# Two product banks lent to the score visits of the w_out stages

## The chip, the cores and the metric

The kernel runs on one core of a Trainium2 chip. The metric is device time in microseconds (us), and the median of the kernel before is 370.91 us over three runs (370.6, 370.91, 370.95). Names: TensorE is PE in the profile (its weight loads are PEld), VectorE is DVE, ScalarE is ACT, GpSimd is POOL, SyncE is SP. PSUM is the memory that TensorE writes; here it is used as eight banks, each holding 512 float32 values on each of the 128 partitions.

## The reference

Squared-ReLU attention is followed by a two-layer network with squared ReLU. There are 8 batches, 12 heads, 448 positions and a head width of 64; the model width is 768 and the inner width 2048.

```python
scores = scale * np.matmul(q, k.transpose(0, 1, 3, 2))
attn = np.maximum(scores, 0.0) ** 2 / S
attn_out = np.matmul(attn, v)
x = attn_out.transpose(0, 2, 1, 3).reshape(B * S, H * D)
r = np.maximum(x @ w_in, 0.0)
return (r * r) @ w_out
```

## The kernel before

**Work and stages.** Attention is cut into 24 units of four heads (three units for each batch), and each unit into 7 score tiles of 128 x 896. A score tile is four quarter-array matmuls at 448 columns (`score`, matmul at L262). ScalarE takes it out of PSUM with a ReLU (L266), VectorE squares it (L369), and when a unit has its seven tiles an AV unit of 28 quarter-array matmuls (`av_unit`, L317) multiplies them by v; ScalarE evicts its result into x (L323).

The first two batches go through w_in as plain products (`h_group`, L409), six matmuls for each of 16 column groups. Then stages alternate: a w_out stage for each pair of batches (four of them, with 3, 4, 3 and 4 groups: 14 in all), and between them the w_in stage of the next pair, with two periods for each batch (12 periods in all).

**A w_in period** (`h_period`, matmuls at L538) is a seven-product scheme on two sets, 14 products of six matmuls. Each set s has two accumulators, X (index 0) and Y (index 1). The tuple `order` names for each product its set, its number in the scheme, its accumulator, whether it starts afresh, and what is done at its end. Counted from 0:

- product 0: set 0, X, copied by ScalarE (L475); 1: set 1, X, copied;
- 2: set 0, Y, summed by VectorE (`plus`, L481); 3: set 0, X, copied; 4: set 1, X, copied; 5: set 1, Y, summed;
- 6: set 0, Y, copied; 7: set 0, X, summed; 8: set 1, X, copied; 9: set 1, Y, summed;
- 10 and 11: sets 0 and 1, X, evicted by ScalarE with a ReLU (L490); 12 and 13: sets 0 and 1, Y, summed by VectorE.

Squares of g by VectorE (L487) lie between. A product that isn't fresh goes on adding into what its accumulator holds.

**A w_out group** (`o_groups`, matmuls at L725) is a seven-product scheme for two row tiles, with products of eight matmuls and two accumulators, X and Y. Its list of products, counted from 0, is (accumulator, fresh, left, right, end):

```python
(X, True, lambda: tile_of(rows[0])[:, LO], b11, end1),
(Y, True, lambda: tile_of(rows[0])[:, HI], b21, end2),
(X, False, lambda: ss[2], t2, end6),
(Y, True, lambda: ss[1], t1, end5),
(X, False, lambda: ss[3], t3, end7),
(X, False, lambda: tile_of(rows[1])[:, HI], nt4, end4),
(Y, False, lambda: ss[4], b22, end3))
```

After product 0 ScalarE copies X (L627); after 1 VectorE adds that copy to Y (L632); after 2 ScalarE copies X; after 3 nothing is read; after 4 ScalarE copies X and VectorE adds the copy to Y; after 5 ScalarE evicts X (L675); after 6 VectorE adds to Y. The next group's product 0 is placed between products 4 and 5. At the end of a stage that another follows, a w_in product of the next stage stands in that place. In the last group of all, product 5 has an accumulator Z in the other pair, and product 6 is cut in two (L707).

**PSUM.** The pool `s_p` holds two score slots of two banks each. The pools in `big`, called mma and mmb, have two buffers of one bank each. `mm_tile(i)` takes a fresh one-bank tile from pool i, and without i from the two pools in turn. A w_in period takes set 0's X and Y from one pool and set 1's from the other. A w_out group n takes both of its accumulators from pool n % 2, so that the other pool is free from the end of the group before until the next group's product 0.

**Order.** The order of instructions on each engine is the order in which the code issues them, and the framework puts in the semaphore waits from what each tile is read and written by. The main loop at the end walks a list `steps` of matmuls with their assumed costs and keeps a `clock`; a list of `events` has due times. In front of a product, where `edge` is true, events that are due are fired. A `visit` is one such event: it issues two score tiles, and an AV unit after the first tile if one is due. 21 visits for each of the last three pairs of batches are spread evenly by due time over the stretch ahead of the w_in stage that needs them. VectorE's squares wait in a list `due` and are put by assumed times of TensorE and VectorE (`fill`, `flush`).

Of the kernel before, what the change touches and what calls it, by code (L numbers as in the profile page):

```python
# [12 lines left out]
FP32 = mybir.dt.float32  # L13
# [5 lines left out]
def kernel(  # L19
# [12 lines left out]
    NT, DM = out.shape  # L32
# [10 lines left out]
    P = 128  # L43
    J = 7
    PW = S // J
    NU = 3
    NUN = B * NU
# [23 lines left out]
    PSUM = bass.MemoryType.PSUM  # L71
# [122 lines left out]
    def slot(dtype, third=False):  # L194
        return (third_p if third else s_p).tile(
            [P, 2, 2048 // mybir.dt.size(dtype)], dtype, name="slot", tag="slot")
# [54 lines left out]
    now = [0]  # L251
    avt = [None]

    def score(t, times=1, third=False):
        n, j = divmod(t, J)
        qT, kT = qkt[n]
        ps = slot(FP32, third)
        for hh in list(range(2)) * times:
            r = slice(64 * hh, 64 * hh + 64)
            for hp in range(2):  # L260
                c = slice(64 * hp, 64 * hp + 64)
                nc.tensor.matmul(  # L262
                    ps[c, hh, 0:S], lhsT=kT[r, j, c], rhs=qT[r, :, c],
                    start=True, stop=True)
        at = at_p.tile([P, 2, S], FP16, name="at", tag="at")
        nc.scalar.activation(out=at, in_=ps[:, :, 0:S], func=AF.Relu, scale=SK)  # L266
        ats[t] = at
        seen[t] = now[0]
# [29 lines left out]

    unit = [NU]

    def av_unit():

        n = unit[0]
        if n == NUN or seen.get(n * J + J - 1, 10 ** 6) >= now[0]:
            return
        unit[0] += 1
        flush(rest=False)
        at_pe[0] += 1.33
        b, u = divmod(n, NU)
        vt = vts[n]  # L310
        ps = slot(FP32)
        for j in range(J):
            at = ats.pop(n * J + j)
            for hp in range(2):
                r = slice(64 * hp, 64 * hp + 64)
                for hh in range(2):
                    nc.tensor.matmul(  # L317
                        ps[64 * hh:64 * hh + 64, hp, 0:S],
                        lhsT=vt[r, hh, j * D:(j + 1) * D], rhs=at[r, hh, :],
                        start=(j == 0), stop=(j == J - 1))  # L320
        if u == 0:
            xts[b] = x_p.tile([P, NM, S], FP16, name="xt", tag="xt")
        nc.scalar.activation(  # L323
            out=xts[b][:, 2 * u:2 * u + 2, :], in_=ps[:, :, 0:S],
            func=AF.Copy, scale=CX)

    def prefetch(m):
        if m >= NUN:
            return
        dma_transpose(m)  # L330
        if m > NPE:
            load_v(m)
        if m + 2 < NUN:
            load_qk(m + 2)
# [10 lines left out]
    def flush(rest=True):  # L345
        for d in (due, due_g) if rest else (due,):
            while d:
                put(d)

    def put(d):  # L350
        ready, cost, fn, _ = d.popleft()
        at_ve[0] = max(at_ve[0], at_pe[0], ready) + cost
        fn()

    def fill(until):
        for d in (due, due_g):
            while d and max(at_ve[0], at_pe[0], d[0][0]) + d[0][1] <= until:
                put(d)
# [8 lines left out]
    def square(at, lag=0.0):  # L367
        due.append((at_pe[0] + lag, 0.54,
                    lambda: nc.vector.tensor_mul(at, at, at), 0))  # L369

    def visit(tiles):
        now[0] += 1
        for t in tiles:
            if t % J == 0 and t >= NPE * J:
                prefetch(t // J + 2)
        for t in tiles[:1]:
            score(t)
        av_unit()
        for t in tiles[1:]:
            score(t)  # L380
        at_pe[0] += 0.19 + 0.19 * len(tiles)
        for i, t in enumerate(tiles):
            square(ats[t], 0.6 + 0.85 * i)
# [2 lines left out]
    gts: dict = {}  # L386
    mm_no = [0]

    def mm_tile(i=None, dtype=FP32):
        if i is None:  # L390
            mm_no[0] += 1
            i = mm_no[0] % len(big)
        return big[i].tile(
            [P, 2048 // mybir.dt.size(dtype)], dtype, name="mm", tag="mm")

    def g_of(b):
        if b // 2 not in gts:
# [42 lines left out]
    def sums_x(b, i):  # L440
        xt = xts[b]
        lo, hi = slice(0, NH), slice(NH, NM)
        b11, b12, b21, b22 = (xt[:, lo, 0:Q], xt[:, lo, Q:S], xt[:, hi, 0:Q],
                              xt[:, hi, Q:S])
        now_ve(0.42)
        if i != 2:
            t = late["xs"].tile([P, NH, Q], FP16, name=f"x{i}", tag=f"x{i}")
            xsum[b, i] = t
        if i == 0:
            nc.vector.tensor_sub(t, b12, b11)  # L450
        elif i == 1:
            nc.vector.tensor_sub(t, b22, xsum[b, 0])
        elif i == 2:
            nc.vector.tensor_sub(b12, b22, b12)
        else:
            nc.vector.tensor_sub(t, b21, xsum[b, 1])
# [139 lines left out]
    def o_groups(groups, then):  # L596
# [5 lines left out]
        def group(n, rows, last):  # L602
# [7 lines left out]
            def needs(k):  # L610

                return max(2 * p + (tb > 2) for p, tb in groups[k]
                           if (p, tb) not in saved)

            def ahead(i, k=n):
                if k < len(groups) and i not in sets[k]:
                    flush_g(needs(k))
                    sums(i, groups[k], sets[k])
# [95 lines left out]
            def step(k, f):  # L714
                acc, fresh, left, right, end = products[k]
                if last and k == 5:
                    acc, fresh = Z, True

                def run():
                    if f == 0 and fresh and k != 3:  # L720
                        acc[:] = [mm_tile((n + (k == 5)) % 2)]
                    if f == 0 and k == 0:
                        ahead(1)
                        ahead(2)
                    nc.tensor.matmul(  # L725
                        acc[0][:, 0:HALF], lhsT=left()[:, f], rhs=right[:, f],
                        start=(fresh and f == 0),
                        stop=(f == KH - 1), skip_group_check=not fresh)
                    if f == KH - 1:
                        end()  # L730
                        if k < 4 and n + 1 < len(groups):
                            some = sum(d[3] <= needs(n + 1) for d in due_g)
                            for _ in range(-(-some // (4 - k))):
                                put(due_g)
                        fill(at_pe[0] + AFTER[k])
                return run

            ls = [[(0.1625, step(k, f), ((2 if k == 5 else True) if f == 0 else False))
                   for f in range(KH)] for k in range(7)]
            if last:  # L740
                ls[6] = [(0.0825, step3(z, f), False) for z in range(2) for f in range(KH)]
# [2 lines left out]
        def pre(i):  # L744
            sums(i, groups[0], sets[0])

        lists = [group(n, rows, rows == LAST) for n, rows in enumerate(groups)]
        for n, ls in enumerate(lists):
            for k in range(7):
# [26 lines left out]
    NB0 = NU * J  # L776
    ps = slot(FP32, True)
# [3 lines left out]
    def s(t, times=2):  # L781
# [73 lines left out]
    load_qk(7)  # L855
    first.close()
    big.append(ctx.enter_context(tc.tile_pool(
        name="mma", bufs=2, space=PSUM, reuse_waits="tile")))

# [2 lines left out]
    def some(part):  # L864
        for _, fn, _ in part:
            fn()
# [6 lines left out]
    some(f1[0:4])  # L873
    rounds.close()
    big.append(ctx.enter_context(tc.tile_pool(
        name="mmb", bufs=2, space=PSUM, side="right", reuse_waits="tile")))
    some(f0[4:6])
    visit([NB0, NB0 + 1])

# [6 lines left out]
    events = []  # L886
# [22 lines left out]
    for m in (6, 7):  # L909
        events.append((T_H + (1 + 3 * (m - 6)) * T_G, lambda m=m: prefetch(m)))  # L910
    at0 = T_H + 8 * T_G
    for pr in range(1, B // 2):
        t0 = 2 * NB0 * pr
        end = begin[pr] + T_S - 6.5
        gap = (end - at0) / 21
        for i in range(21):
            ts = [t0 + 2 * i, t0 + 2 * i + 1]
            events.append((at0 + i * gap, lambda ts=ts: visit(ts), True))
        at0 = end
        for i in range(4):  # L920
            events.append((begin[pr] - 6 + i, lambda b=2 * pr, i=i: sums_x(b, i)))
    events.append((at0 + 0.3, lambda: visit([]), True))

    def pre(pr, i):
        def run():
# [29 lines left out]
                steps += periods[b, i0]  # L955
        steps += outs[pr][0]

    clock, last = 0.0, 0.0
    ev = deque(sorted(events, key=lambda e: e[0]))
    for cost, fn, edge in steps:  # L960
        fired = 0
        while ev and edge and ev[0][0] <= clock + (1.6 if edge == 2 and not fired else 1e-3):
            if len(ev[0]) == 3:
                if clock < last + 1.5:
                    break
                last = clock
            ev.popleft()[1]()
            fired += 1
        if fn is not None:
            at_pe[0] += cost  # L970
            fn()
        clock += cost
# [31 lines left out]
```

## Time and profile before

| what | value |
| --- | --- |
| median of three runs | 370.91 us |
| profiled execution, its own time | 370.7 us |
| its span | 368.9 us |
| granted TensorE clock | 0.998 |
| TensorE busy | 359.6 us |
| VectorE busy | 265.4 us |
| ScalarE busy | 247.5 us |
| GpSimd busy | 107.1 us |

The span is the time from the first to the last instruction that the profiler saw; the profiled execution's own time is 1.8 us longer. A row of a group of instructions gives the source line, the engine, the operation, what it writes and reads, how often, its busy time and the mean of one. Some rows that later steps use:

| line | engine and what it does | times | mean, ns |
| --- | --- | --- | --- |
| L266 | ACT, eviction of a score tile, 128 x 896 | 168 | 925 |
| L323 | ACT, eviction of an AV unit, 128 x 896 | 21 | 917 |
| L475 | ACT, copy in a w_in period, 128 x 448 | 72 | 552 and 554 |
| L481 | DVE, sum in a w_in period, 128 x 448 | 72 | 622 and 619 |
| L627 | ACT, copy in a w_out group, 128 x 384 | 42 | 492 and 494 |
| L632 | DVE, sum in a w_out group, 128 x 384 | 44 | 542 and 556 |
| L369 | DVE, square of a score tile, 128 x 896 | 147 | 617 |

In the timeline, an entry begins with its start in us and its length in us; a matmul's end is modelled, so the start of the next matmul tells better when TensorE was free. In brackets stand the idle time before an instruction and what ended it.

### The profile page before, as it was taken

How to read it: one execution, taken by the hardware profiler on the slowest of the kernel's cores; microseconds unless marked ns; L12 is line 12 of the kernel's file. 1: busy time of each engine (PE TensorE's matmuls, PEld its weight loads, DVE VectorE, ACT ScalarE, POOL GpSimd, SP SyncE). 2: the span in 40 equal slices, each digit the busy share in tenths (PEclk: the TensorE clock that was granted, in tenths of full speed). 3: DMA queues.
4: the chain of work that ended last, by engine and by line, in shares of the span. 5: the costliest groups of instructions: out<-in, count | busy, mean ns of one | idle time of the engine just before them, and what ended most of it. 6: DMA issues, size and time to landing. Idle time of an engine off the chain costs nothing.

```text
span 368.9 us, 8720 instructions
## 1 busy us (share of the span) xinstructions
PE 359.6 (97%) x3588; PEld 230.3 (62%) x3588; DVE 265.4 (72%) x470; ACT 247.5 (67%) x371; POOL 107.1 (29%) x128
## 2 busy tenths in 40 slices
PE   8899999999999999999999999999999999999994
PEld 3644445445555778875555588786555689976663
DVE  2997677997777787788585766989766686884442
ACT  3988894787676989876556588886765885532220
POOL 8545521846553155531225045140000000000001
PEclk9999999999999999999999999999999999999999
DMA  8999999999999999967699899692323300003333
GB/s 115 191 207 203 205 204 162 161 158 165 190 166 127 184 101 98 115 93 62 140 166 105 159 155 86 88 116 37 65 71 88 85 3 2 2 0 85 87 92 81
DMA packets 121159, 42.64 MB, mean 116 GB/s; under 512 B 100832, under 2 KB 117760, under 8 KB 121120
## 3 DMA queue, kind: packets, MB, share of 16 engines
q0 software_dynamic: 82912, 23.01, 62.3%
q1 hardware_dynamic: 38048, 18.98, 25.7%
q8 instruction: 28, 0.46, 0.5%
q10 hardware_dynamic: 160, 0.10, 0.1%
q14 instruction: 11, 0.09, 0.1%
HBM read 45.61 MB, written 11.01 MB: 153 GB/s over the span
## 4 chain that ended last, share of the span: by engine, by line
PE 90%; ACT 3%; DVE 3%; issue 2%; DMA 1%; POOL 0%; POOLq 0%; ACTq 0%
PE mm L725 34%; PE mm L538 27%; PE slot L262 10%; PE mm L409 9%; PE slot L317 7%; ACT at L266 3%; DMA k<-in_k_dram 1%; DVE at L297 1%; PE avt L280 1%; PE slot L238 1%; PE mm L238 0%; DVE at L369 0%; DVE xt L292 0%; ACT u L627 0%; DVE osb L632 0%
## 5 line engine op out<-in xcount | busy, mean ns | idle before, releaser
L266 ACT ACTIVATE at<-slot 128x896 f16<-128x896 f32 x168 | 145.8, 925 | 22.2 <-PE slot L262 22.2
L369 DVE TENSOR_TENSOR at<-at 128x896 f16<-128x896 f16 x147 | 87.1, 617 | 9.7 <-ACT at L266 9.6
L109 POOL DMA_DIRECT2D qs<-in_q_dram x36 | 35.3, 983 | 113.7 <-DMA qT<-qs 106.2
L725 PEld LDWEIGHTS <-s 128*128 128x128 f16 x440 | 41.5, 98 | 32.7 <-issue 3.6
L262 PE MATMUL slot<-qT,kT 64*64 64x448 f16 x744 | 56.8, 361 | 1.9 <-ACT at L266 1.4
L538 PEld LDWEIGHTS <-w 128*128 128x128 f16 x576 | 54.3, 98 | 5.1 <-issue 4.3
L538 PE MATMUL mm<-xt,w 128*128 128x224 f16 x432 | 48.9, 259 | 0.0
L725 PEld LDWEIGHTS <-g 128*128 128x128 f16 x336 | 31.7, 98 | 24.1 <-issue 4.7
L538 PEld LDWEIGHTS <-ws 128*128 128x128 f16 x432 | 40.3, 98 | 4.7 <-issue 4.7
L632 DVE SCALAR_TENSOR_TENSOR osb<-mm,u 128x384 f32<-128x384 f32 (+1 forms) x30 | 16.2, 542 | 36.4 <-ACT u L627 24.0
L725 PE MATMUL mm<-b,g 128*128 128x384 f16 x224 | 40.7, 326 | 0.0
L725 PE MATMUL mm<-b,s 128*128 128x384 f16 x216 | 39.6, 326 | 0.2 <-DVE s L594 0.2
L409 PE MATMUL mm<-xt,w 128*128 128x448 f16 x192 | 39.8, 354 | 0.0
L725 PE MATMUL mm<-t,s 128*128 128x384 f16 x224 | 39.3, 326 | 0.0
L109 POOL DMA_DIRECT2D ks<-in_k_dram x36 | 35.1, 976 | 9.4 <-DMA b<-in_moe_w_out_dram 5.8
L262 PEld LDWEIGHTS <-kT 64*64 64x64 f16 x744 | 19.0, 104 | 28.7 <-issue 23.3
L561 POOL DMA_DIRECT2D out_dram<-osb x2 | 1.1, 563 | 119.6 <-DVE osb L632 119.6
L627 ACT ACTIVATE u<-mm 128x384 f32<-128x384 f32 x28 | 13.8, 492 | 31.6 <-PE mm L725 27.1
L538 PE MATMUL mm<-x,ws 128*128 128x224 f16 x288 | 34.1, 259 | 0.0
L481 DVE CUSTOM_DVE_ANT_0 g<-mm,m 128x448 f16<-128x448 f32 x36 | 22.4, 622 | 15.1 <-PE mm L538 7.3
L317 PE MATMUL slot<-at,vt 64*64 64x448 f16 x588 | 31.9, 350 | 0.2 <-DVE at L369 0.2
L409 PEld LDWEIGHTS <-w 128*128 128x128 f16 x192 | 17.1, 98 | 19.2 <-issue 5.1
(76 smaller groups left out, 399.7 us busy)
## 6 DMA issues: line engine op xcount, KB each, us to landing
out_dram<-osb SPq DMA_DIRECT2D x52, 192.0 KB, 3.0
vt<-in_v_dram POOLq DMA_DIRECT2D x24, 224.0 KB, 6.2
qs<-in_q_dram POOLq DMA_DIRECT2D x36, 112.0 KB, 4.6
ks<-in_k_dram POOLq DMA_DIRECT2D x36, 112.0 KB, 5.0
w<-in_moe_w_in_dram POOLq DMA_DIRECT2D x8, 384.0 KB, 11.9
b<-in_moe_w_out_dram POOLq DMA_DIRECT2D x4, 768.0 KB, 17.1
q<-in_q_dram POOLq DMA_DIRECT2D x6, 224.0 KB, 7.9
k<-in_k_dram POOLq DMA_DIRECT2D x6, 224.0 KB, 8.3
```

What stands on the lines that cost most here:

```text
L109: nc.gpsimd.dma_start(out=t[:, :, hh, :], in_=heads(src, n)[:, hh].rearrange("p (j d) -> p j d", d=D))
L238: nc.tensor.transpose(pss[i][64 * hh:64 * hh + 64, i if n < 4 else 0, j * P:(j + 1) * P], src[:, hh, j * D:(j + 1) * D], ident)
L262: nc.tensor.matmul(ps[c, hh, 0:S], lhsT=kT[r, j, c], rhs=qT[r, :, c], start=True, stop=True)
L266: nc.scalar.activation(out=at, in_=ps[:, :, 0:S], func=AF.Relu, scale=SK)
L317: nc.tensor.matmul(ps[64 * hh:64 * hh + 64, hp, 0:S], lhsT=vt[r, hh, j * D:(j + 1) * D], rhs=at[r, hh, :], start=(j == 0), stop=(j == J - 1))
L369: lambda: nc.vector.tensor_mul(at, at, at), 0))
L409: nc.tensor.matmul(cell[0][:, 0:S], lhsT=w1[f // 4][:, m, (f % 4) * P:(f % 4 + 1) * P], rhs=xts[b][:, m, :], start=(m == 0), stop=(m == NM ...
L481: nc.vector._custom_dve(TENSOR_ADD_SAT, out=gs(s, hi, right), in0=acc(s, y), in1=keep[s, nm], s0=3.4e38, s1=0.0)
L538: nc.tensor.matmul(XY[s][y][:, r * Q:(r + 1) * Q], lhsT=left(k, i0 + 2 * s + r, m), rhs=right(k, m), start=(fresh and r == 0 and m == 0), ...
L627: nc.scalar.activation(out=t, in_=X[0][:, 0:HALF], func=AF.Copy, scale=CO)
L632: nc.vector.scalar_tensor_tensor(out=osb[row][:, c], in0=acc[0][:, 0:cc.stop - cc.start], scalar=CO, in1=keep[nm][:, cc], op0=ALU.mult, op ...
L725: nc.tensor.matmul(acc[0][:, 0:HALF], lhsT=left()[:, f], rhs=right[:, f], start=(fresh and f == 0), stop=(f == KH - 1), skip_group_check=n ...
```

## The change

The change has three parts. First, each pair of product banks is no longer a pool of two one-bank buffers but **one tile of two banks**, taken once for the whole kernel. `mm_tile` returns one half of it, and the halves alternate (`side`). Second, `visit`, `score` and `av_unit` take an optional place `spare`: if an AV unit is due it goes there, otherwise the visit's first score tile does. Third, the visits of the last three pairs are no longer events at fixed times. The main loop counts the tiles that are issued (`tile_no`) against the plan (`planned`), and fires a visit at an edge where the count has fallen to the plan. At the edges of products 2 and 4 of a w_out group, a visit has three tiles and gets the pair that the group doesn't use, as soon as it is at most 1.5 tiles ahead of the plan; elsewhere it has two, as before.

In the built programs, there are 76 calls of `visit` before (63 of them and one without tiles in the last three pairs) and 67 after. 18 of the 67 have three tiles, and all 18 are in w_out stages. The number of matmuls doesn't change, nor does the order of transfers on the SP and POOL queues.

```diff
-    def score(t, times=1, third=False):
+    def score(t, times=1, third=False, ps=None):
...
-        ps = slot(FP32, third)
+        ps = slot(FP32, third) if ps is None else ps
...
-    def av_unit():
+    def av_due():
         n = unit[0]
-        if n == NUN or seen.get(n * J + J - 1, 10 ** 6) >= now[0]:
+        return n < NUN and seen.get(n * J + J - 1, 10 ** 6) < now[0]
+
+    def av_unit(ps=None):
+        if not av_due():
             return
...
-        ps = slot(FP32)
+        ps = slot(FP32) if ps is None else ps
...
-    def visit(tiles):
+    def visit(tiles, spare=None):
...
         for t in tiles[:1]:
-            score(t)
-        av_unit()
+            score(t, ps=None if av_due() else spare)
+        av_unit(spare)
...
+    side = [0, 0]
     def mm_tile(i=None, dtype=FP32):
...
-        return big[i].tile(
-            [P, 2048 // mybir.dt.size(dtype)], dtype, name="mm", tag="mm")
+        side[i] ^= 1
+        return big[i][:, side[i]].bitcast(dtype) if dtype != FP32 else big[i][:, side[i]]
...
-            ls = [[(0.1625, step(k, f), ((2 if k == 5 else True) if f == 0 else False))
+            edges = {2: (n + 1) % 2, 4: (n + 1) % 2}
+            ls = [[(0.1625, step(k, f),
+                    ((edges.get(k), k == 5) if f == 0 else False))
                    for f in range(KH)] for k in range(7)]
...
     big.append(ctx.enter_context(tc.tile_pool(
-        name="mma", bufs=2, space=PSUM, reuse_waits="tile")))
+        name="mma", bufs=1, space=PSUM, reuse_waits="tile")).tile(
+            [P, 2, 512], FP32, name="mma", tag="mma"))
...
     big.append(ctx.enter_context(tc.tile_pool(
-        name="mmb", bufs=2, space=PSUM, side="right", reuse_waits="tile")))
+        name="mmb", bufs=1, space=PSUM, side="right", reuse_waits="tile")).tile(
+            [P, 2, 512], FP32, name="mmb", tag="mmb"))
...
-        gap = (end - at0) / 21
-        for i in range(21):
-            ts = [t0 + 2 * i, t0 + 2 * i + 1]
-            events.append((at0 + i * gap, lambda ts=ts: visit(ts), True))
+        plan.append((at0, end, t0))
...
-    events.append((at0 + 0.3, lambda: visit([]), True))
...
+        while ev and edge and ev[0][0] <= clock + 1e-3:
+            ev.popleft()[1]()
+        if edge and clock >= plan[0][0]:
+            pair, soon = edge if edge is not True else (None, False)
+            ahead = tile_no - planned(clock)
+            if tile_no == NT:
+                if unit[0] < NUN and clock > last + 1.5:
+                    visit([])
+                    last = clock
+            elif pair is not None and ahead <= 1.5 and clock > last + 1.25:
+                n = min(3, NT - tile_no)
+                visit(list(range(tile_no, tile_no + n)), big[pair])
+                tile_no += n
                 last = clock
-            ev.popleft()[1]()
-            fired += 1
+            elif ahead <= (1.5 if soon else 0.0) and clock > last + 1.5:
+                n = min(2, NT - tile_no)
+                visit(list(range(tile_no, tile_no + n)))
+                tile_no += n
+                last = clock
```

The new functions and lines move the ones below them: in the kernel after, L323 is L327, L369 is L373, L409 is L418, L475 is L484, L481 is L490, L490 is L499, L538 is L547, L594 is L603, L627 is L636, L632 is L641, L675 is L684 and L725 is L734.

## Prediction

> **What bounds the kernel now.** I read the page first, then the waits of TensorE, the chain that ended last, and two stretches of the timeline.
>
> ```profile
> PE 359.6 (97%) x3588; PEld 230.3 (62%) x3588; DVE 265.4 (72%) x470; ACT 247.5 (67%) x371; POOL 107.1 (29%) x128
> ...
> PE 90%; ACT 3%; DVE 3%; issue 2%; DMA 1%; POOL 0%; POOLq 0%; ACTq 0%
> ```
>
> TensorE (PE) is busy in 97% of the span and is 90% of the chain. This is all that its matmuls wait for:
>
> ```profile
> PE slot L262 <- ACT at L266: 1.4, 6, 0.3
> PE slot L200 <- DVE zeros L158: 1.2, 1, 1.2
> PE slot L238 <- ACT at L266: 0.5, 2, 0.2
> PE slot L262 <- DVE kT L215: 0.2, 1, 0.2
> PE mm L725 <- DVE s L594: 0.2, 1, 0.2
> PE slot L317 <- DVE at L369: 0.2, 1, 0.2
> ```
>
> That is 3.7 us, and the product lines L538 and L725 have 0.2 of it. So the time is TensorE's own work: the change gains what it takes off TensorE and loses whatever makes TensorE wait. The chain prices a visit, and the wake-up of TensorE after another engine:
>
> ```profile
> 80.31 2.71 PE mm L725 x16
> 83.02 0.50 PE slot L262 x8
> 83.52 2.71 PE mm L725 x16
> ...
> 204.64 0.61 DVE s L594
> 205.25 0.05 issue
> 205.30 1.47 PE mm L725 x8
> ```
>
> Two score tiles take 0.50 us, and the 16 matmuls beside them 2.71. The timeline of the last w_out stage, which has no visits, shows how evictions lie beside products today:
>
> ```profile
> 338.97 2.76 PE L725 MATMUL mm<-t,s 128*128 128x384 f16 x16
> 339.23 0.56 DVE L632 SCALAR_TENSOR_TENSOR osb<-mm,m 128x384 f32<-128x384 f32 x1 [0.80 <-PE mm L725]
> 340.52 0.49 ACT L627 ACTIVATE u<-mm 128x384 f32<-128x384 f32 x1 [3.46 <-PE mm L725]
> 341.57 1.46 PE L725 MATMUL mm<-b,s 128*128 128x384 f16 x8
> ```
>
> These 16 matmuls are products 2 (in bank X) and 3 (in bank Y) of a group; they take 341.57 - 338.97 = 2.60 without a pause. VectorE reads product 1 out of Y while product 2 runs in X, and ScalarE reads product 2 out of X while product 3 runs in Y. The same in a w_in period:
>
> ```profile
> 322.67 0.74 PE L538 MATMUL mm<-x,ws 128*128 128x224 f16 x6
> 323.24 1.31 PE L538 MATMUL mm<-xt,w 128*128 128x224 f16 x12
> 323.44 0.54 ACT L475 ACTIVATE m<-mm 128x448 f32<-128x448 f32 x1 [0.61 <-PE mm L538]
> 324.12 0.62 DVE L481 CUSTOM_DVE_ANT_0 g<-mm,m 128x448 f16<-128x448 f32 x1 [0.53 <-ACT m L475]
> ```
>
> Product 6 ends at 323.24 in Y; its eviction starts 0.20 later, while product 7 already runs in X.
>
> [...]
>
> **Part 1: fewer visits.** The built orders have 76 visits before and 67 after, with the same matmuls (3588). A tile is 0.19 us (28 matmuls, seven tiles' worth, are 1.32 us in the chain). A visit's own cost is 0.50 - 2 x 0.19 = 0.12 at its entry and 2.71 - 2.60 = 0.11 at its exit: 0.23. Nine fewer: **-2.1 us**. The two 0.2 us waits in products and AV units lie in crowded places that the new plan thins out: -0.4.
>
> **Part 2: one tile for two banks.** Before, every accumulator is a tile of its own, from a pool of two. After, each pair is one tile for the whole kernel, and `mm_tile` returns a half. The framework sets waits by tile. I followed each wait in the two built programs to the instruction that brings the semaphore to the awaited count: before, no product waits on a reader of another bank; after, 123 products at L547 (the old L538), 58 at L734 (old L725) and 23 at L418 (old L409) wait on the reader of **the other half of their pair**. So a product that ran beside its neighbour's eviction now waits for it. These are no new instructions, only the cover that is gone. Behind the waiting matmul stands everything that TensorE has left.
>
> Price of such a wait, when the eviction belongs to the product just ahead: by ScalarE 0.20 (release, above) + 0.55 (rows L475: 552 and 554 ns) + 0.05 (wake-up) = 0.80; by VectorE 0.20 + 0.62 (rows L481) + 0.05 = 0.87. With one product of 0.576 between, 0.22 and 0.29.
>
> w_in period, 14 products. Product 3 waits for VectorE's sum of 2 (0.87); 5, 7 and 9 for ScalarE's copies of 4, 6 and 8 (3 x 0.80); 11 for the sum of 9 (0.29); 13 for relu of 11 (0.22); the next period's 0 and 1 for the sums of 12 and 13 (together 0.30). Product 2's wait for the copy of 0 is covered, since 1 was late; 4, 6, 8, 10 and 12 find their releases done. Sum 4.08. In VectorE's new order squares that wait for products 10 and 11 stand ahead of the last two sums: about 0.45 more. 12 periods: 12 x 4.53 = **+54.4**.
>
> w_out group, 7 products; the next group's product 0 runs in the other pair between 4 and 5. Product 2 waits for VectorE's sum of 1: 0.26 + 0.56 + 0.05 = 0.87. Product 3 waits for ScalarE's copy of 2: 0.25 + 0.49 + 0.05 = 0.79. Product 5 waits for copy and sum after 4: 0.26 + 0.49 + 0.14 + 0.56 + 0.05 = 1.50, of which the next group's product covers 1.30: 0.20. Product 6 waits for the copy of 5: 0.20 + 0.50 + 0.05 = 0.75. Sum 2.61; 14 groups: **+36.5**. In each of the four stages the first product 1 follows its product 0 directly (4 x 0.74 = 3.0), and in three the last group has a w_in product of 0.576 where 1.30 was (3 x 0.73 = 2.2): **+5.2**.
>
> First batches (L409): each half is freed one group of 1.14 us ahead, and an eviction takes 0.80. Between 0 and 4 us; I take +1.
>
> **Part 3: visits among these waits.** A visit ahead of a waiting product is hidden in its wait; but ScalarE works in order, and a visit's evictions (0.925 each) stand ahead of the next copy. In w_out, three tiles ahead of product 2 hide its 0.87, and then 2.78 us of evictions delay the copy that product 3 now waits for: 0.35 + 2.78 + 0.54 = 3.67 after the visit's start instead of 2.1 + 0.79, some 0.8 more: even. Ahead of product 4, with about half of the 18 visits of three, the copy and the sum that product 5 waits for end some 0.8 later with nothing hidden: 9 x 0.8 = 7; the two-tile visits hide about 1: **+6**. In w_in stages 25 visits either hide some 0.6 (ahead of 3, 5, 7, 9) or push a copy back by up to 1.2 (ahead of 4, 10): near even, with squares in front of VectorE's sums **+4**. Not seen in any trace: bounds from -12 (each visit hidden wherever it can be) to +20 (each pushes one eviction).
>
> The three-tile visit itself needs no wait: spare is free when it starts (last reader one product back or more), and its eviction ends before the pair's next product. POOL and SP queues get the same transfers in the same order around moved visits; their landing is far from the chain (no DMA in it after the start).
>
> **Sum**, on the profiled execution's 370.7 us (span 368.9 and 1.8 around it; the runs' median is 370.91, as good as equal): -2.1 - 0.4 + 54.4 + 36.5 + 5.2 + 1 + 6 + 4 = +104.6, so **475 us**. The release latency may be 0.1 off in 100 direct waits (10 us), and part 3 has its bounds.
>
> **Rivals.**
> - *Half the waits are covered* (423 us, half of 104): visits and late evictions overlap more than the walk through one period shows, as ScalarE and VectorE have over 28% of the span free. Against it: the last four w_out groups and most of the last three w_in periods have no visits at all, and there nothing can cover.
> - *The waits don't bind, only the visits count* (370.7 - 2.5 = 368.2 us, not slower). Place: products 3, 5, 7, 9 and 2, 3, 6. It decides if the release a product waits for belongs to an earlier reader than I took, so that it comes before TensorE arrives: with more than 0.80 us of other TensorE work between, no wait is left. The counts in the built program speak against it.
> [...]
>
> **Numbers.** Main case 0.86, half covered 0.07, no binding 0.03, pile-up 0.04. The main case's own bounds are 440 to 500; inside lies some 0.8 of all, so that is the range. Within 0.2% is about what the runs can tell from no change. Slower by more than 0.2%: main, half and pile-up, 0.97; within: 0.01; faster: 0.02.
>
> **What would show it.** In the after profile, the waits of TensorE list L547 on ACT L484 and DVE L490 and L734 on ACT L636 and DVE L641, together some 90 to 100 us where it was 0.2; PE's share near 77% with busy time near 358; a timeline in which product 7 starts 0.8 after product 6 ends; the last w_out stage, 37 us from 327 on, some 10 us longer. The visit count's saving shows as 67 entries. Wrong would be: those waits under 20 us in sum, or a granted clock under 0.95.

## Result and profile after

The kernel after takes **462.19 us** (median of four runs, 462.13 to 463.85) against 370.81 us before (also four runs): a ratio of 1.2476, 95% interval 1.2447 to 1.2504. It is slower by 91.4 us; the forecast was 475 us, range 440 to 500. The profiled execution has 462.18 us, a span of 460.4 us and a granted clock of 0.998.

The page of the kernel after, parts 1 and 4:

```profile
PE 376.8 (82%) x3588; PEld 232.5 (50%) x3588; DVE 269.1 (58%) x470; ACT 250.1 (54%) x371; POOL 107.1 (23%) x128
...
PE 14%; DVE 4%; ACT 3%; issue 1%; ACTq 0%; DVEq 0%
```

The same 3588 matmuls now fill 82% of a longer span. The chain, which before was TensorE nearly throughout, could be followed back only to 349.7 us; its shares are of the whole span and add up to 22%, so it can't be compared with the one of before.

The waits of TensorE's matmuls in the kernel after. Each row names what the matmul writes and its line, after the arrow the instruction whose end it waited for, and then the us in total, the times and the longest. The ten largest:

```profile
PE mmb L547 <- ACT u L484: 15.7, 19, 1.5
PE mma L547 <- DVE g L490: 8.8, 12, 0.8
PE mma L734 <- ACT u L636: 8.4, 8, 1.2
PE mmb L734 <- ACT u L636: 6.2, 6, 1.2
PE mma L547 <- ACT m L484: 6.2, 11, 0.7
PE mmb L547 <- DVE g L490: 4.9, 18, 0.3
PE mma L734 <- ACT osb L684: 4.8, 8, 0.7
PE mma L734 <- DVE osb L641: 4.4, 5, 1.3
PE mmb L734 <- DVE osb L641: 3.6, 5, 1.3
PE mmb L734 <- ACT osb L684: 3.0, 5, 0.7
```

Every entry is a product (L547 in a w_in period, L734 in a w_out group) that waits for a copy, a sum or an eviction out of the same pair. Before, all product lines together waited 0.2 us; these ten are 66.0 us. They aren't the whole loss: when TensorE stops, the tail of its last matmul counts as busy (0.74 for the 0.57 of product 6 in the next lines), and busy time rose by 376.8 - 359.6 = 17.2 us with the same matmuls (the last section comes back to this).

A w_in period without a visit, kernel after (start, length, engine; in brackets the idle time before and what ended it):

```profile
401.73 0.74 PE L547 MATMUL mma<-x,ws 128*128 128x224 f16 x6
402.03 0.62 DVE L490 CUSTOM_DVE_ANT_0 g<-mmb,m 128x448 f16<-128x448 f32 x1 [2.87 <-PE mmb L547]
...
402.56 0.54 ACT L484 ACTIVATE m<-mma 128x448 f32<-128x448 f32 x1 [1.46 <-PE mma L547]
403.16 0.73 PE L547 MATMUL mma<-xt,w 128*128 128x224 f16 x6 [0.69 <-ACT m L484]
403.73 0.74 PE L547 MATMUL mmb<-xt,w 128*128 128x224 f16 x6
```

These are products 6, 7 and 8, with the sum of product 5 and the copy of product 6. Product 6 starts at 401.73 and needs 0.57; product 7 would have followed at 402.30. It starts at 403.16, 0.06 after the copy of product 6 ended (402.56 + 0.54), so the wait costs 0.86. Before, product 7 started 0.20 ahead of that copy. Product 8 is in the other pair, whose last reader, the sum of product 5, ended at 402.65 (402.03 + 0.62); it too starts only at 403.73, 0.57 behind product 7. So here the wait of one product held up the one behind it.

The last w_out stage, which has no visits, kernel after:

```profile
424.27 0.56 DVE L641 SCALAR_TENSOR_TENSOR osb<-mmb,m 128x384 f32<-128x384 f32 x1 [0.67 <-PE mmb L734]
424.75 0.68 DVE L603 TENSOR_TENSOR s<-g,g 128x1024 f16<-128x1024 f16 x1
424.88 1.46 PE L734 MATMUL mmb<-t,s 128*128 128x384 f16 x8 [0.65 <-DVE osb L641]
425.35 0.69 DVE L603 TENSOR_TENSOR s<-g,s 128x1024 f16<-128x1024 f16 x1
426.43 0.49 ACT L636 ACTIVATE u<-mmb 128x384 f32<-128x384 f32 x1 [5.01 <-PE mmb L734]
426.97 1.46 PE L734 MATMUL mmb<-t,s 128*128 128x384 f16 x8 [0.63 <-ACT u L636]
428.27 1.46 PE L734 MATMUL mmb<-b,s 128*128 128x384 f16 x8
```

Products 2 and 3, which before were one row of 16 matmuls in 2.60 us, are two rows with a copy between: from 424.88 to 428.27 are 3.39 us. Product 2 itself had to wait for the sum at 424.27.

Stage lengths, from the starts of the stages' first products in the timelines (us; a w_out stage here includes the one w_in product that stands among its last products, and the last stage runs to the end of its last matmul):

| stage | before | after | joined tile alone (first experiment) |
| --- | --- | --- | --- |
| first batches | 55.6 | 56.3 | 57.1 |
| w_out 1, 2, 3 | 38.4, 48.0, 36.8 | 49.7, 60.6, 46.2 | 44.9, 56.7, 42.7 |
| w_in 1, 2 | 43.7, 43.7 | 59.2, 58.0 | 59.3, 59.9 |
| w_in 3 (four visits) | 36.4 | 54.7 | 54.8 |
| w_out 4 (no visits) | 36.6 | 47.2 | 47.2 |

The change also moves visits between stages: its first w_out stage has 26 score tiles and 4 AV units where the kernel before has 20 and 3 there. So its column can be set against the one before stage by stage only in the last two rows, which have the same tiles in both kernels; the joined tile alone has the visits of before in every row.

### The profile page after: what moved, and what is told of

It reads as the page before. It is cut to its first block, busy times and chain, and to the rows that moved or that the text cites. A ratio compares the mean times of both kernels' runs of the same rounds, so it can differ in the third digit from the quotient of the medians.

```text
span 460.4 us, 8759 instructions
## 1 busy us (share of the span) xinstructions
PE 376.8 (82%) x3588; PEld 232.5 (50%) x3588; DVE 269.1 (58%) x470; ACT 250.1 (54%) x371; POOL 107.1 (23%) x128
## 5 line engine op out<-in xcount | busy, mean ns | idle before, releaser
L266 ACT ACTIVATE at<-slot 128x896 f16<-128x896 f32 x156 | 134.9, 924 | 19.8 <-PE slot L262 19.7
L373 DVE TENSOR_TENSOR at<-at 128x896 f16<-128x896 f16 x147 | 86.4, 618 | 19.2 <-ACT at L266 18.9
L547 PEld LDWEIGHTS <-w 128*128 128x128 f16 x576 | 54.7, 97 | 37.0 <-issue 36.1
L734 PEld LDWEIGHTS <-s 128*128 128x128 f16 x440 | 41.6, 97 | 62.6 <-issue 37.6
L547 PEld LDWEIGHTS <-ws 128*128 128x128 f16 x432 | 40.7, 97 | 24.3 <-issue 24.0
L734 PEld LDWEIGHTS <-g 128*128 128x128 f16 x336 | 32.3, 98 | 32.1 <-issue 12.4
L547 PE MATMUL mmb<-xt,w 128*128 128x224 f16 x216 | 26.5, 258 | 13.4 <-ACT u L484 10.1
L547 PE MATMUL mma<-xt,w 128*128 128x224 f16 x216 | 26.5, 258 | 8.9 <-ACT m L484 6.2
L490 DVE CUSTOM_DVE_ANT_0 g<-mma,m 128x448 f16<-128x448 f32 x24 | 15.0, 625 | 30.6 <-PE mma L547 17.5
L734 PE MATMUL mma<-t,s 128*128 128x384 f16 x128 | 23.4, 325 | 9.8 <-ACT u L636 8.4
L641 DVE SCALAR_TENSOR_TENSOR osb<-mma,u 128x384 f32<-128x384 f32 (+1 forms) x18 | 9.8, 546 | 35.6 <-ACT u L636 23.2
L496 DVE TENSOR_TENSOR g<-g 128x896 f16<-128x896 f16 x48 | 29.1, 618 | 2.6 <-ACT g L499 2.6
L484 ACT ACTIVATE m<-mma 128x448 f32<-128x448 f32 x24 | 13.1, 546 | 30.5 <-PE mma L547 30.5
L734 PE MATMUL mma<-b,s 128*128 128x384 f16 x128 | 23.4, 326 | 4.8 <-ACT osb L684 4.8
L418 PEld LDWEIGHTS <-w 128*128 128x128 f16 x192 | 17.4, 98 | 19.8 <-issue 5.6
L734 PE MATMUL mma<-b,g 128*128 128x384 f16 x128 | 23.4, 326 | 2.4 <-ACT g L431 0.9
L547 PE MATMUL mma<-x,ws 128*128 128x224 f16 x144 | 17.7, 259 | 8.1 <-DVE g L490 8.1
```

The costliest lines, as they stand in the source:

```text
L418: nc.tensor.matmul(cell[0][:, 0:S], lhsT=w1[f // 4][:, m, (f % 4) * P:(f % 4 + 1) * P], rhs=xts[b][:, m, :], start=(m == 0), stop=(m == NM ...
L484: nc.scalar.activation(out=t, in_=XY[s][y][:, 0:S], func=AF.Copy)
L490: nc.vector._custom_dve(TENSOR_ADD_SAT, out=gs(s, hi, right), in0=acc(s, y), in1=keep[s, nm], s0=3.4e38, s1=0.0)
L496: lambda: nc.vector.tensor_mul(g, g, g), b))
L547: nc.tensor.matmul(XY[s][y][:, r * Q:(r + 1) * Q], lhsT=left(k, i0 + 2 * s + r, m), rhs=right(k, m), start=(fresh and r == 0 and m == 0), ...
L641: nc.vector.scalar_tensor_tensor(out=osb[row][:, c], in0=acc[0][:, 0:cc.stop - cc.start], scalar=CO, in1=keep[nm][:, cc], op0=ALU.mult, op ...
```

## Experiments

Theory: one tile for two banks makes each product wait for the reader of its neighbour bank. Rivals: the visits of three tiles and their evictions cause the loss; the plan of visits does; the fixed banks in turn come free later than a pool's buffers.

**The joined tile alone, in the kernel before.**

```diff
-        return big[i].tile(
-            [P, 2048 // mybir.dt.size(dtype)], dtype, name="mm", tag="mm")
+        side[i] ^= 1
+        return big[i][:, side[i]].bitcast(dtype) if dtype != FP32 else big[i][:, side[i]]
...
-        name="mma", bufs=2, space=PSUM, reuse_waits="tile")))
+        name="mma", bufs=1, space=PSUM, reuse_waits="tile")).tile(
+            [P, 2, 512], FP32, name="mma", tag="mma"))
...
```

The lines left out do the same for mmb.

> The kernel before with one part of the change alone: each pair of product banks is one tile of two halves; visits, plan and slots are as before. Theory (waits on the reader of the other half): 370.8 plus the waits of 12 periods, 14 groups and the stage edges, about what the whole change cost, and 2 us more since the nine visits aren't saved: 464 us, 455 to 472, with TensorE waits on L539 and L726 of 60 us or more in the table. Rival (the three-tile visits and their evictions cause a good share): under 450 us. Rival (the new plan of visits causes it): 371 us.

Measured: 453.25 us, ratio 1.2236 (1.2213 to 1.2258), 82.5 us over its before (370.78). The main part of the loss needs neither the new plan nor a visit of three. The time lies 2 us under the range that I gave: the whole change costs 9 us more than this part, where I had expected it to be 2 us cheaper.

**The same banks in the same turn, each a tile of its own, in the kernel before.**

```diff
+    def four(pool, nm):
+        return [pool.tile([P, 512], FP32, name=f"{nm}{i}", tag=f"{nm}{i}") for i in range(2)]
...
-        return big[i].tile(
-            [P, 2048 // mybir.dt.size(dtype)], dtype, name="mm", tag="mm")
+        side[i] ^= 1
+        return big[i][side[i]].bitcast(dtype) if dtype != FP32 else big[i][side[i]]
...
```

The lines left out take both pairs with `four`.

> The kernel before with the change's way of handing out banks (two fixed banks for each pair, handed out in turn), but each bank is a tile of its own. Theory (the joined tile is the cause): 370.8 us, within 1 us of before, and no product waits for a reader of another bank. Rival (fixed banks in turn come free later than a pool's buffers, so the rotation itself makes the waits): well above 380 us.

Measured: 370.72 us, ratio 0.9999 (0.9991 to 1.0007). What products and AV units wait for is what it was before:

```profile
PE mmb L730 <- DVE s L599: 0.2, 1, 0.2
PE slot L317 <- DVE at L369: 0.2, 1, 0.2
```

This differs from the kernel of the first experiment in nothing but whether two banks are one tile or two. So the joining is the cause, and neither the fixed banks nor their turn.

**One pair joined, the other not.** The edit is that of the first experiment for mma and of the second for mmb.

> The kernel before, with the banks of one pair (mma) joined to one tile of two halves and the other pair's banks a tile each. Theory (each wait on the other half's reader adds up by itself): a w_in period keeps the waits of products 2, 3, 7, 12 and 0 (0.22 + 0.87 + 0.80 + 0.22 + 0.29, with squares 0.3 more: 2.7, times 12 = 32); of the 14 w_out groups the 8 on this pair keep 2.61 each, and the stage edges 4.5: 25. In the kernel with both pairs joined, the same walk gave 97 and the run 82.5, as visits hide some: 0.85 x 57 = 48, so 419 us, 412 to 426. Rival (the waits of the two pairs lie on top of each other, so one pair gives nearly all): 440 us or more. Rival (it needs both pairs, one alone is covered by the other's products): under 390 us.

Measured: 420.48 us, ratio 1.1341 (1.1326 to 1.1357), 49.8 us over before, where 48 were expected. The walk through the products, scaled by the 0.85 that the run with both pairs joined gave, has the size as well as the sign: one pair is 57 of 97 us in the walk and 49.8 of 82.5 in the runs. All its waits for copies, sums of products and evictions are on mma; the largest:

```profile
PE mma L544 <- DVE g L487: 10.4, 16, 0.8
PE mma L544 <- ACT m L481: 8.0, 13, 1.0
PE mma L731 <- DVE osb L638: 4.1, 7, 0.7
PE mma L731 <- ACT osb L681: 3.8, 6, 0.7
```

**The whole change with separate tiles**, the free pair's two banks evicted by two ScalarE instructions of 448 columns.

```diff
+        if isinstance(ps, list):
+            for hh in range(2):
+                nc.scalar.activation(
+                    out=at[:, hh], in_=ps[hh][:, 0:S], func=AF.Relu, scale=SK)
...
```

The lines left out do the same for an AV unit and make each bank a tile, as above.

> The whole change, but each bank is a tile of its own; where a score tile or an AV unit goes to the free pair, its two banks are evicted by two ScalarE instructions of 448 columns instead of one of 896. Theory: the waits are gone, nine visits of 0.23 us are saved, and two evictions of 0.55 in place of one of 0.92 cost nothing, as ScalarE has slack: 368.3 us, 367.5 to 369.5. Rival (three tiles at once make waits of their own behind ScalarE's queue, ahead of products 3 and 5): 372 us or more.

Measured: 373.46 us, ratio 1.0076 (1.0061 to 1.0092). My theory fell here, and the rival came true: even without the joined tile the visits of three cost time. The timeline of this kernel, ahead of a product 4 (the profiled execution took 375.22 us; in it TensorE also waits 1.8 us for transfers of k and v before 17 us):

```profile
87.93 0.63 DVE L385 TENSOR_TENSOR at<-at 128x896 f16<-128x896 f16 x1 [0.17 <-ACT at L271]
88.27 0.38 PE L262 MATMUL mmb<-qT,kT 64*64 64x448 f16 x4
88.47 0.68 DVE L619 TENSOR_TENSOR s<-g 128x1024 f16<-128x1024 f16 x1
88.49 0.55 PE L262 MATMUL slot<-qT,kT 64*64 64x448 f16 x8
88.69 0.98 ACT L268 ACTIVATE at<-mmb 128x448 f16<-128x448 f32 x2 [0.41 <-PE mmb L262]
89.07 0.69 DVE L619 TENSOR_TENSOR s<-g,s 128x1024 f16<-128x1024 f16 x1
89.21 1.47 PE L750 MATMUL mma<-b,s 128*128 128x384 f16 x8 [0.17 <-DVE s L619]
```

At 87.93 VectorE squares the third tile of the visit before, as soon as ScalarE has evicted it. Only then, at 88.47, comes the sum s that product 4 reads; product 4 starts at 89.21, 0.06 after its end. The evictions of three tiles hold up a square, and the square holds up a sum that doesn't need it. By the starts, product 4 is 0.24 late here; the same wait makes two others, at 173.47 and 197.28, 1.03 late. Two evictions in place of one are hardly a burden: 0.98 for both halves against 0.92 for the whole.

**The plan alone**: the kernel above with two tiles in every visit, none in the free pair.

```diff
-                n = min(3, NT - tile_no)
-                visit(list(range(tile_no, tile_no + n)), big[pair])
+                n = min(2, NT - tile_no)
+                visit(list(range(tile_no, tile_no + n)))
```

> As the kernel of the split spare banks, but every visit has two tiles and none uses the free pair: the new plan of visits alone. Theory: as many visits as before, 370.8 us, 370 to 371.5. Rival (it is the plan, with visits moved to other products, that saves or costs time): as far from 370.8 as the split spare is, 368.3 or less, or 372 or more.

Measured: 370.31 us, ratio 0.9990 (0.9983 to 0.9996), as expected. The new plan by itself costs nothing and saves 0.5 us: the two small waits of 0.2 us, product on sum and AV unit on square, are gone from its table.

**Sums of g ahead of squares**, in the kernel with separate tiles.

```diff
-        while due and due[0][0] <= max(at_ve[0], at_pe[0]) + 0.3:
-            put(due)
```

> The kernel with the split spare banks (e3), with one edit: a sum of g for a w_out group is put into VectorE's queue at once, not behind squares of score tiles that are assumed to be ready. Theory (e3 loses because the sum that product 4 reads stands behind squares that wait for ScalarE's evictions of three tiles): those waits go and the nine saved visits show: 369.3 us, 368.3 to 370.3. Rival (the late squares then stop the AV unit, or ScalarE's queue holds product 5 anyway): 373 us, as e3.

Measured: 371.71 us, ratio 1.0028 (1.0018 to 1.0038). This is neither the theory's range nor the rival's 373. The matmuls' waits for sums (2.5 us on L750 before the edit) are gone, and 1.75 us of the 3.1 us that this kernel had lost to the plan alone came back. So both were partly right; most of what remains stands in its waits:

```profile
PE mma L748 <- ACT u L650: 1.4, 2, 0.7
...
PE mmb L748 <- ACT u L650: 0.7, 1, 0.7
```

Three times product 5 of a stage's last group, where only a short w_in product is between, waits for a copy behind three evictions, and starts 0.87 late.

**No visit of three ahead of product 4 in the last group of a stage**, in the kernel above (`del edges[4]` there).

> The kernel of e6, without visits of three ahead of product 4 in the last group of a stage, where only a w_in product of 0.57 stands between products 4 and 5. Theory (what e6 still loses are the three waits of product 5, 0.7 us each in the table, for a copy behind three evictions): those go, two more visits come at 0.23: 371.7 - 2.4 + 0.5 = 369.8 us, 369 to 370.4, faster than before. Rival (the tiles moved to other visits bring waits of their own): 371 us or more.

Measured: 370.6 us, ratio 0.9991 (0.9984 to 0.9998). The three waits are gone and no product waits in the table, yet the time is 0.2 us above the range I gave and no better than the plan alone, though seven visits fewer should be worth 1.6 us. So some 1.9 us are lost, and the trace shows where most of them are. Eight products that should have followed the work ahead of them at once start about 0.15 us late, where the plan alone has none. One of them, a product 4:

```profile
191.05 2.77 PE L748 MATMUL mma<-t,s 128*128 128x384 f16 x16
191.64 1.73 ACT L271 ACTIVATE at<-slot 128x896 f16<-128x896 f32 x2
193.23 0.52 ACT L650 ACTIVATE u<-mma 128x384 f32<-128x384 f32 x1
193.81 1.46 PE L748 MATMUL mma<-b,s 128*128 128x384 f16 x8
```

Products 2 and 3 need 2.60 us, to 193.65; product 4 starts at 193.81, 0.06 after the end of the copy of product 2, which came behind three evictions. All eight (five products 4 and three products 5) start 0.05 to 0.06 after such a copy: 1.2 us together. They aren't in the table of waits, as the modelled end of the matmuls ahead (191.05 + 2.77 = 193.82 here) leaves no gap. And one AV unit waits 0.44 us for a late square. So ScalarE's queue behind a visit of three still reaches TensorE where no wait is listed. No version tried beats the kernel before by more than 0.1%.

**Visits of three ahead of product 2 alone, and ahead of product 4 alone**, in the kernel after, with the joined tile.

```diff
-            edges = {2: (n + 1) % 2, 4: (n + 1) % 2}
+            edges = {2: (n + 1) % 2}
```

> The whole change, with three-tile visits ahead of product 2 of a w_out group alone (10 of them; 71 visits from the first w_out stage's plan on, by the same count of the whole kernel 4 to 5 fewer than before). Theory of the prediction (a visit of three ahead of product 2 hides one wait and lengthens the next, even): about as the joined tile alone, 453 less 1 for saved visits: 452 us, 450 to 455. Rival (three evictions ahead of a copy cost 0.6 or more wherever they stand): 458 us or more.

> The whole change, with three-tile visits ahead of product 4 of a w_out group alone (10 of them). Theory of the prediction (a visit of three ahead of product 4 pushes the copy and the sum that product 5 waits for by 0.8 and hides nothing): 453 + 8 - 1 = 460 us, 457 to 463. Rival (it is the visits ahead of product 2 that cost): 453 us or less.

Measured: 454.94 us (ratio 1.2272, 1.2256 to 1.2289) and 457.50 us (1.2342, 1.2323 to 1.2361). Against the joined tile alone, less 1.1 us for five saved visits, ten visits of three ahead of product 2 cost 2.8 us and ten ahead of product 4 cost 5.4. The order of the two is as predicted; the sizes are 0.3 and 0.5 us a visit where I had 0 and 0.8. The expectations' own ranges hold both, the first at its high end and the second at its low end. These two kernels have the new plan as well, which moves tiles between stages and wasn't run alone with the joined tile, so the sizes are those of whole kernels.

## Why the prediction was right, by its own steps

**What bounds the kernel** held: all that was lost is TensorE waiting, and the engines that it waits for have less than 60% to do (VectorE 58%, ScalarE 54%).

**Part 2, the joined tile,** held in its mechanism by the first two experiments together, and in its walk by the stages with few or no visits. The last w_out stage was to lose 4 x 2.61 + 0.74 = 11.2 us and lost 47.2 - 36.6 = 10.6. A single wait for ScalarE was 0.80 and measured 0.86 in the lines above. The last w_in stage was to lose 4 x 4.53 = 18.1 us and lost 54.7 - 36.4 = 18.3, but so close an agreement is luck. Its last two periods have no visit; by the starts of their first products (383.05 and 396.25, then the w_out stage at 409.21) they took 13.2 and 13.0 us where 14 products need 8.05, and so lost 5.2 and 4.9 against the walk's 4.53. Among others, product 2, which I had called covered, waits 0.27 in the last one, and product 11 waits 0.41 in place of 0.29. The two periods with visits lost only the other 8.2.

**The term that was mis-sized is part 3**, the visits among the waits, in both of its signs. With the joined tile alone, the visits are those of before, and they hide far more than "near even":

| term | on record | joined tile alone |
| --- | --- | --- |
| w_in waits, and visits there | 54.4 + 4 | 15.6 + 16.2 + 18.4 = 50.2 |
| w_out waits and stage edges | 36.5 + 5.2 | 6.5 + 8.7 + 5.8 + 10.6 = 31.6 |
| first batches | 1 | 1.5 |

The w_in stages with visits throughout lost 15.6 and 16.2 where the third lost 18.4, and the first three w_out stages lost 21.0 where the walk without visits gives 41.7 - 11.2 = 30.5. So against the walk the visits of two came to about -4 in w_in, where I had +4, and to about -10 in w_out, where I had -1. Since a w_in period without visits loses nearer 5.0 than 4.53, what they hid in w_in is more than 4, and the walk was short there. This is seen where a visit stands ahead of a product that waits anyway; joined tile alone:

```profile
149.33 0.74 PE L539 MATMUL mmb<-xt,w 128*128 128x224 f16 x6
...
150.00 0.38 PE L262 MATMUL slot<-qT,kT 64*64 64x448 f16 x4
150.10 0.54 ACT L476 ACTIVATE u<-mmb 128x448 f32<-128x448 f32 x1 [1.40 <-PE mmb L539]
150.21 1.49 PE L317 MATMUL slot<-at,vt 64*64 64x448 f16 x28
...
151.82 0.75 PE L539 MATMUL mmb<-x,ws 128*128 128x224 f16 x6
```

Product 8 ends at 149.9, and the copy that product 9 waits for runs from 150.10 to 150.64, wholly beside a visit with an AV unit; product 9 follows the visit without a wait.

In the other direction, the visits of three were to cost 9 x 0.8 = 7 us. The whole change measured 462.2 - 453.2 = 9 us above the joined tile alone, and if the nine saved visits are worth their 2.1, the visits of three cost 11. One of them ahead of product 2, kernel after:

```profile
100.33 0.38 PE L262 MATMUL mma<-qT,kT 64*64 64x448 f16 x4
...
101.04 1.46 PE L734 MATMUL mmb<-t,s 128*128 128x384 f16 x8
101.57 1.72 ACT L266 ACTIVATE at<-slot 128x896 f16<-128x896 f32 x2
...
103.17 0.51 ACT L636 ACTIVATE u<-mmb 128x384 f32<-128x384 f32 x1
...
103.73 1.46 PE L734 MATMUL mmb<-t,s 128*128 128x384 f16 x8 [1.23 <-ACT u L636]
```

The copy of product 2 comes at 103.17, behind the evictions; product 3 starts 103.73 - 100.33 = 3.40 after the visit's start (3.67 on record). The step held in this place. But on average such visits weren't even: the ten in the experiment with product 2 alone cost 0.3 each.

Set against the walk as recorded, the visits together came to about -14 + 11 = -3 us where +10 was forecast, and these are the 13 us by which 475 was too high. That it isn't 17 is luck too: the gain from hiding was set 17 us too small, and 4 us of this were made up by a cost of the visits of three that was also set too small.

**Part 1, the saving** of 0.23 us a visit: in the traces before and of the plan alone a visit costs 0.22 to 0.23 by the starts beside it. That it reaches the end time is not shown: with separate tiles, nine or seven visits fewer brought nothing net. The other 0.4 us of part 1, the two waits that the new plan thins out, fit the plan alone: they are gone there and it is 0.5 us faster. **"The three-tile visit itself needs no wait"** was true for its own banks and wrong for what it does to others: it delays squares and copies, and by these products 4 and 5 even where each bank is a tile of its own.

**The rivals.** "The waits don't bind" fell with the first experiment. "Half the waits are covered" would have been 423 us; about 15% is covered (82.5 of 97 are left). A pile-up of evictions ahead of copies, 0.04 among the chances, did not come: the time is below the forecast, TensorE's longest wait was 1.5 us, and the granted clock was 0.998.

**What was to show it.** The lines that should wait do, but the table's sum is nearer to 70 us than to the 90 to 100 I gave, and TensorE is at 82% with 376.8 us busy, not 77% with 358: a stopped TensorE's tails count as busy.

## What to carry to other kernels

A framework that places waits from what a tile is read and written by may treat a tile of two banks as one thing; here it did, and the joined tile alone cost 82.5 us. Before banks are joined to lend them out, follow the waits of the built program to their releasing instructions and look for a neighbour's reader; keeping a tile for each bank and evicting in two instructions avoided these waits here, at 0.06 us for each eviction (0.98 against 0.92). And count what a burst of tiles does to the work that stands behind it on the engines that take them out: here, with separate tiles, a copy behind three evictions made product 5 start 0.87 late in three places, and a sum behind the square of a visit's third tile made product 4 start 0.24 late in one place and 1.03 in two.

## What the runs showed that was not expected

A profile's busy time for TensorE grew with its stops: 17.2 us more for the same 3588 matmuls at the same clock. The list of waits has 106 on product lines; 17.2 us over these is 0.16 each, and product 6 in the lines above counts 0.74 for work of 0.57 before it stops. So a table of TensorE's waits understates what the waits cost, here by about a fifth of the loss (17.2 of 91.4 us).
